# A spectral filter mixed with a token MLP: first weights on ScalarE's queue, two roots on ScalarE, second biases later, slots by their planes, last block in three pieces

## The chip, the cores and the metric

The kernel runs on one core of one Trainium2 chip. The metric is the device time of one execution in microseconds (us); the time before is the median of three runs, 129.3 us (129.15 to 129.92). The profile is of one execution, with all times counted from its first instruction. PE is TensorE's matmul stream, PEld its weight loads, DVE is VectorE, ACT is ScalarE, POOL is GpSimd, SP is SyncE, which here only issues transfers. A name with q (SPq, ACTq) is an engine's queue of issues.

## What is computed

The input x has 2048 rows of 512 columns in bf16. Two branches work on it and a gate per row mixes them.

```python
def _A_ref(x, w_r, w_i):
    X = rfft2(x.astype(float32)) * (w_r + 1j * w_i)
    return irfft2(X, s=(S, D)).astype(bfloat16)

def _B_ref(x, w1, b1, w2, b2):
    h = _layernorm(x, axis=-1)                       # (x - mean) / sqrt(var + 1e-5)
    u = _gelu(einsum("bsd,sf->bdf", h, w1) + b1)     # F = 1792
    y = einsum("bdf,fs->bds", u, w2) + b2
    return y.transpose(0, 2, 1)

g = _sigmoid((x * gate_w).sum(-1, keepdims=True))
return g * a + (1 - g) * b
```

## The kernel before, in words

The 2048 rows are 16 blocks of 128, one row to a partition. A block has the number b (0 to 15); "block 3 of x" is the one with b = 3.

**The MLP branch** is all matmuls of 128x128 weights against 512 columns. The first layer has 14 tiles of 128 features (ft), each the sum over the 16 blocks; 8 of them are made first, block after block as the normed blocks `hn` appear (`mm1`, L276, accumulators `u1`, weights `w1a`), the other 6 later from `w1b` (L446). The second layer makes each of 16 output blocks from 14 matmuls (L456, weights `w2t`, output `yb`); the last block is made apart, in two halves of columns (L785). ScalarE turns a first-layer tile into `gl` with gelu and the bias column `b1f` (L342), and evacuates each finished output block to `tbv` with the gate's scale and a bias `ombb2`, which is made from `b2f` (L436). The two bias vectors are loaded as rows into one tile `brow` (30 rows, L120 and L121) and turned to columns by one small matmul against a unit matrix (L240), which ScalarE copies to `bcol` (L294).

**The layer norm** of a block: DVE takes statistics (`bstat`, L247) and aggregates them (`aggr`, L254), adds epsilon (L256), POOL takes the power -1/2 (`rstd`, L259), and DVE scales the block (`norm_dve`, L272) for blocks 0 to 5; from block 6 on ScalarE scales (L268).

**The spectral branch** folds x by symmetries on DVE (L375 to L425) into planes `YA` and `YB`, for the even and the odd frequency groups A and B. PE transforms along the tokens (`token`, L504 and L505; 4 steps for a group, number r, each from planes 2r and 2r+1), ScalarE copies the result out (L506), PE transforms along the columns (`dpass`, L513), ScalarE copies again to `csA` or `csB` (L515), DVE applies the spectral weights and sums (L520 to L550, results `PMA` and `PMB`), and PE transforms back (`inv_tok`, L642, and `inv_d`, L658) with ScalarE copying between (L614). DVE unfolds the result (L690 to L758) into `ap`, which is added to the stored output by accumulating transfers from POOL's queue (L763) or, for blocks 12 to 14, by DVE (L772). The tables of sines (`TD`, `TA`) are made on the chip: POOL writes counters, DVE forms angles `md` and masks them (L205, L191), ScalarE takes sines (L194, L197).

**What sets the order.** Each engine runs its instructions in the order in which the code names them. A generator, `products`, holds the 96 + 210 = 306 MLP matmuls that follow the first eight tiles. `fill(n)` puts n of them into PE's order; `fill_to(t)` puts them until a planned clock reaches t. The clock starts at 33.2 and goes on by 0.2165 for each product and by `spent` for the transforms (0.87 a token step, 0.44 a column step). The constants `T_TA`, `T_TB`, `T_IA`, `T_IB`, `T_Y` (L24) are the planned times at which tokens A, tokens B, inverse A, inverse B and the unfolding come. They decide only the order on PE, and with it the order of ScalarE's evacuations, not a wait.

**The loads** are issued by SP in the order of L118 to L139: block 0 of x, then x and `w1a` blocks in turn, the gate's row `gwb`, the rest of `w1a`, `w1b` and the spectral weights. ACT's queue issues only the two bias rows. A transfer signals one of eight completion counters, taken in turn, and an issue waits for the earlier transfer that used its counter.

**The start of PE** is a row of warm-up matmuls on zeros (L241), nine of them, with the bias matmul behind the seventh. `pw` and `pb` share the two slots of the tag "mm" with `u1_6` and `u1_7`; the eighth tile's first matmul waits for the bias copy.

Of the kernel before, what the change touches and what calls it, by code (L numbers as in the profile page):

```python
# [20 lines left out]
NFT = 14  # L21
FT1 = 8
NDVE = 6
T_TA, T_TB, T_IA, T_IB, T_Y = 42.2, 55.4, 69.8, 82.6, 99.8  # L24
PI_IN = 3.1415925
INV_SCALE = 2.0 / (512.0 * 2048.0)
C1 = float(np.cos(np.pi / 8))
# [16 lines left out]
def kernel(  # L44
# [13 lines left out]
    nc = tc.nc  # L58
# [5 lines left out]
    small = ctx.enter_context(tc.tile_pool(name="small", bufs=1))  # L64
# [9 lines left out]
    def pair(name):  # L74
        return psum.tile([P, 2, 512], F32, tag="pair", name=name, bufs=3)
# [11 lines left out]
    w1b, w2t = {}, {}  # L87

    def load_x(b0, b1):
        nc.sync.dma_start(out=xh[b0 // 8][:, b0 % 8:(b1 - 1) % 8 + 1], in_=xv[:, b0:b1])  # L90

    def load_w1a(b0, b1):
        nc.sync.dma_start(out=w1a[b0 // 4][:, b0 % 4:(b1 - 1) % 4 + 1], in_=w1v[:, b0:b1, 0:FT1 * P])

    def load_w(i):

# [19 lines left out]
        nc.sync.dma_start(out=w2t[c][:], in_=w2v[:, :, c * 256:(c + 1) * 256])  # L116

    load_x(0, 1)  # L118
    brow = small.tile([NFT + NB, P], BF16, name="brow")
    nc.scalar.dma_start(out=brow[0:NFT], in_=B_b1.rearrange("(ft f) -> ft f", f=P))  # L120
    nc.scalar.dma_start(out=brow[NFT:NFT + NB], in_=B_b2.rearrange("(b a) -> b a", a=P))  # L121
    for b in range(3):
        load_x(b + 1, b + 2)
        load_w1a(b, b + 1)
    load_x(4, 6)
    load_w1a(3, 4)
    load_x(6, 8)
# [4 lines left out]
    load_w1a(8, 12)  # L132
    gwb = small.tile([P, D], BF16, name="gwb")
    nc.sync.dma_start(out=gwb[:], in_=gate_w[None, :].to_broadcast([P, D]))
    load_w1a(12, 16)
    load_w1b(0, 4)
    load_w1b(1, 5)
# [2 lines left out]

    warm = small.tile([P, P], BF16, name="warm")
    nc.vector.memset(warm[:], 0.0)
    consts = small.tile([P, 5], F32, name="consts")
    nc.vector.memset(consts[:, 0:1], -PI_IN)
    nc.vector.memset(consts[:, 1:2], PI_IN)
    nc.vector.memset(consts[:, 2:3], -0.5)  # L146
    nc.vector.memset(consts[:, 3:4], 0.0)
    nc.vector.memset(consts[:, 4:5], 1536.0)
    c_mpi, c_pi, c_mhalf = consts[:, 0:1], consts[:, 1:2], consts[:, 2:3]

    lrow = H(4, [P, 3, P], "lrow", F32)
# [9 lines left out]
    iota(lrow[:, 0:2], [[0, 2], [2, P]], 0)  # L161
    iota(lrow[:, 2], [[2, P]], 1)
    nc.gpsimd.memset(lrow[:, 1, 0:1], 256.0)
    ident = small.tile([NFT + NB, NFT + NB], BF16, name="ident")
    idf = small.tile([NFT + NB, NFT + NB], F32, name="idf")
    iota(idf[:], [[1, NFT + NB]], 0, -1)
    nc.gpsimd.tensor_single_scalar(ident[:], idf[:], 0.0, op=Alu.is_equal)
    iota(krow[:, 0], [[8, 2], [16, 64]], 0)
    iota(krow[:, 1], [[16, P]], 6)
# [20 lines left out]
    def mask(m, n):  # L190
        nc.vector.tensor_single_scalar(m, m, n - 1, op=Alu.bitwise_and)  # L191
# [8 lines left out]
    ma = [H(7, [P, 8, P], "ma0", I32), H(8, [P, 8, P], "ma1", I32)]  # L200
    mc = small.tile([P, 1], I32, name="mc")

    def angles_d():
        for v in range(2):
            nc.vector.tensor_scalar(md[:, v], lrow[:], acol[:, 1:2], 768.0 * v, op0=Alu.mult, op1=Alu.add)  # L205
        mask(md[:], 1024)

    def sines_d():
        nsin(TD[:, :, 1], md[:, 1], 1024)
        nsin(TD[:, :, 2], md[:, 0], 1024)  # L210
        psin(TD[:, :, 0], md[:, 0], 1024)
# [23 lines left out]

    pw = bank("pw")
    pb = bank("pb")
    for n in range(9):
        if n == 7:
            nc.tensor.matmul(pb[:, 0:NFT + NB], lhsT=brow[:], rhs=ident[:], start=True, stop=True)  # L240
        nc.tensor.matmul(pw[:].rearrange("p (n k) -> p n k", n=4), lhsT=warm[:],  # L241
                         rhs=warm[:, None, :].to_broadcast([P, 4, P]), start=True, stop=True)
    pu = [pair(f"u1_{i}") for i in range(3)]
# [2 lines left out]
    def bstat(b):  # L246
        nc.vector.bn_stats(out=stats[:, b, :], in_=xh[b // 8][:, b % 8, :])  # L247
# [4 lines left out]
    def aggr(b0, b1):  # L252
        for b in range(b0, b1):
            nc.vector.bn_aggr(out=mv[:, b, :], in_=stats[:, b, :])  # L254
        eng = nc.vector if on_dve(b0) else nc.gpsimd
        eng.tensor_scalar(mv[:, b0:b1, 1], mv[:, b0:b1, 1], 1e-5, 0.0, op0=Alu.add, op1=Alu.add)  # L256
        if not on_dve(b0):
            nc.gpsimd.tensor_scalar(nmr[:, b0:b1], mv[:, b0:b1, 0], -1.0, 0.0, op0=Alu.mult, op1=Alu.add)
        nc.gpsimd.tensor_tensor(rstd[:, b0:b1], mv[:, b0:b1, 1], c_mhalf.to_broadcast([P, b1 - b0]), op=Alu.pow)  # L259
# [24 lines left out]
    def gacc(b0, b1):  # L284
        for b in range(b0, b1):
            junk = small.tile([P, D], BF16, tag="junk", name="junk")
            nc.scalar.activation(junk[:], prod[b // 8][:, b % 8], ActF.Copy, accum_out=glog[:, b:b + 1])  # L287

    sink = small.tile([P, 1], F32, name="sink")
    nc.scalar.activation(sink[:], consts[:, 2:3], ActF.Sin, bias=c_mpi, scale=0.0)  # L290
    angles_d()
    sines_d()
    bcol = small.tile([P, NFT + NB], F32, name="bcol")
    nc.scalar.copy(bcol[:], pb[:, 0:NFT + NB])  # L294
    b1f, b2f = bcol[:, 0:NFT], bcol[:, NFT:]
    for v in range(2):
        nc.scalar.activation(ma[v][:], krow[:], ActF.Identity, bias=consts[:, 3 + v:4 + v], scale=acol[:, 0:1])
    nc.scalar.activation(mc[:], acol[:, 0:1], ActF.Identity, bias=consts[:, 4:5], scale=1024.0)


    bstat(0)
    aggr(0, 1)
    for b in range(NDVE):
        bstat(b + 1)
        norm_dve(b)
        if b + 1 < NDVE:
            aggr(b + 1, b + 2)
# [162 lines left out]
    def hook(b):  # L470
        store(b)

    clock = [33.2]
    act = [0.0]

    def fill(n):
        for _ in range(n):
            if next(prods, 0) == 0:
                return
            done[0] += 1  # L480
            clock[0] += 0.2165
# [69 lines left out]

    gacc(0, 4)
    fill(16)
    gacc(4, 7)
    fill(16)
    gacc(7, 10)
# [13 lines left out]
        fill(4)  # L570
    fill_to(T_TB)
    ZB = H(6, [P, 4, 4, 2, P], "ZB")
    for r in range(4):
        token(1, r, ZB, YB)
        spent(0.87)
        if r % 2:
            gacc(14 + r // 2, 15 + r // 2)
        fill(2)
    g_ = small.tile([P, NB], F32, name="g_")
    nc.scalar.activation(g_[:], glog[:], ActF.Tanh, scale=0.5)  # L580
# [5 lines left out]
    nc.gpsimd.tensor_mul(ombb2[:], omg[:], b2f)  # L586
    gate["omg"], gate["ombb2"] = omg, ombb2
    csB = H(4, [P, 4, 4, 256], "csB")
    for r in range(4):
        dpass(r, ZB, csB)  # L590
        spent(0.44)
        fill(3)
# [185 lines left out]
    fill(10000)  # L778

    b = NB - 1  # L780
    for h in range(2):
        hs = slice(256 * h, 256 * h + 256)
        y = bank("yb")
        for ft in range(NFT):
            nc.tensor.matmul(y[:, 0:256], lhsT=w2t[b // 2][:, ft, P:2 * P], rhs=gl[:, ft, hs],  # L785
                             start=(ft == 0), stop=(ft == NFT - 1))
        nc.vector.scalar_tensor_tensor(tbv[0][:, b, hs], y[:, 0:256], omg[:, b:b + 1], apl[:, hs],
                                       op0=Alu.mult, op1=Alu.add)
        nc.sync.dma_start(out=out2[b * P:(b + 1) * P, hs], in_=tbv[0][:, b, hs])

# [26 lines left out]
```

## Time and profile before

| | us |
|---|---|
| median of three runs | 129.3 |
| the profiled execution, device time | 129.32 |
| its span, first to last instruction | 127.4 |
| first matmul of `mm1` starts | 5.21 |
| PE's last matmul ends | 123.98 |
| last DVE operation ends | 124.49 |
| PE busy, DVE busy, ACT busy | 121.7, 111.0, 87.1 |

The span leaves out 1.9 us around the program. PE's busy time counts the tail of each matmul too, so that a matmul of 512 columns shows as 0.379 while the next starts 0.216 behind it; starts are the better measure. In a line of the timeline the first number is the start, the second the time covered, and the bracket tells how long the engine sat idle and what ended that. In the list of waits stand the waiting engine and line, what it waited for, the total, the times and the longest. A matmul's weight load (PEld) runs ahead of the matmul, so a wait on PEld costs PE only what goes beyond the work still in its queue. Transfers show the time from the start of their issue to their landing where somebody waited for them.

### The profile page before, as it was taken

How to read it: one execution, taken by the hardware profiler on the slowest of the kernel's cores; microseconds unless marked ns; L12 is line 12 of the kernel's file. 1: busy time of each engine (PE TensorE's matmuls, PEld its weight loads, DVE VectorE, ACT ScalarE, POOL GpSimd, SP SyncE). 2: the span in 40 equal slices, each digit the busy share in tenths (PEclk: the TensorE clock that was granted, in tenths of full speed). 3: DMA queues.
4: the chain of work that ended last, by engine and by line, in shares of the span. 5: the costliest groups of instructions: out<-in, count | busy, mean ns of one | idle time of the engine just before them, and what ended most of it. 6: DMA issues, size and time to landing. Idle time of an engine off the chain costs nothing.

```text
span 127.4 us, 2027 instructions
## 1 busy us (share of the span) xinstructions
PE 121.7 (95%) x723; PEld 64.5 (51%) x736; DVE 111.0 (87%) x188; ACT 87.1 (68%) x132; POOL 42.5 (33%) x69
## 2 busy tenths in 40 slices
PE   6999999999999999999999999999999999999990
PEld 2244444444444576447654765477544444444470
DVE  5969998999999999999999999999999999981130
ACT  4930359999897879959992599269764699322420
POOL 7633288998898595000220000000000000530300
PEclk9999999999999999999999999999999999999999
DMA  3799999999999999999399008510012111199691
GB/s 98 228 355 371 376 367 353 279 312 268 217 264 244 249 293 292 290 290 290 78 262 287 25 0 233 184 41 0 0 41 79 49 44 41 41 142 197 101 230 32
DMA packets 34490, 24.03 MB, mean 189 GB/s; under 512 B 5264, under 2 KB 31888, under 8 KB 34480
## 3 DMA queue, kind: packets, MB, share of 16 engines
q1 hardware_dynamic: 32340, 21.01, 60.7%
q0 software_dynamic: 1936, 2.76, 11.9%
q10 hardware_dynamic: 204, 0.14, 0.3%
q8 instruction: 5, 0.08, 0.3%
q14 instruction: 5, 0.04, 0.1%
HBM read 19.15 MB, written 3.67 MB: 179 GB/s over the span
## 4 chain that ended last, share of the span: by engine, by line
PE 53%; DVE 33%; DMA 4%; issue 3%; SPq 2%; POOL 2%; DVEq 0%
PE yb L456 35%; PE ivt L642 5%; DVE stats L247 4%; DMA xa<-in_A_x_dram 4%; DVE prod L280 4%; PE ivd L658 3%; PE u L446 3%; PE yb L785 2%; POOL rstd L259 2%; DVE F L379 2%; DVE s L388 2%; DVE T L375 2%; DVE o L407 2%; DVE F L380 2%; DVE T L376 2%
## 5 line engine op out<-in xcount | busy, mean ns | idle before, releaser
L456 PE MATMUL yb<-gl,w2t 128*128 128x512 bf16 x204 | 46.1, 379 | 0.3
L456 PEld LDWEIGHTS <-w2t 128*128 128x128 bf16 x210 | 20.2, 98 | 22.3
L276 PE MATMUL u<-hn,w1a 128*128 128x512 bf16 x126 | 27.9, 380 | 0.1
L446 PE MATMUL u<-hn,w1b 128*128 128x512 bf16 x91 | 22.4, 379 | 0.2
L436 ACT ACTIVATE tbv<-yb,ombb,omg 128x512 bf16<-128x512 f32 x15 | 11.7, 777 | 14.8 <-PE yb L456 14.8
L763 POOL DMA_DIRECT2D out_dram<-ap x3 | 4.0, 1527 | 51.0 <-DVE ap L758 45.2
L276 PEld LDWEIGHTS <-w1a 128*128 128x128 bf16 x128 | 12.5, 98 | 15.9 <-DMA w1a<-in_B_w_dram 0.9
L446 PEld LDWEIGHTS <-w1b 128*128 128x128 bf16 x96 | 9.1, 98 | 7.9
L287 ACT ACTIVATE junk<-prod 128x512 bf16<-128x512 bf16 x16 | 10.1, 630 | 0.3
L342 ACT ACTIVATE gl<-u,bcol 128x512 bf16<-128x512 f32 x14 | 9.3, 688 | 1.2 <-PE u L446 0.6
L614 ACT CAST R<-ivt 128x1024 bf16<-128x1024 f32 x8 | 7.8, 1038 | 3.4 <-PE ivt L642 3.4
L259 POOL TENSOR_TENSOR rstd<-mv,consts 128x1 f32<-128x1 f32 (+1 forms) x11 | 7.2, 653 | 6.5 <-DVE mv L256 6.3
L614 ACT CAST H<-ivd 128x1024 bf16<-128x1024 f32 x7 | 7.0, 1045 | 0.8 <-PE ivd L658 0.8
L772 DVE TENSOR_TENSOR tbv<-tbv,ap 128x512 bf16<-128x512 bf16 x3 | 1.3, 425 | 6.7 <-ACT tbv L436 6.7
L268 ACT ACTIVATE hn<-xb,nmr,rstd 128x512 bf16<-128x512 bf16 x8 | 6.0, 803 | 1.3 <-POOL nmr L263 1.3
L268 ACT ACTIVATE hn<-xa,nmr,rstd 128x512 bf16<-128x512 bf16 x2 | 1.5, 806 | 7.3 <-DVE nmr L265 7.3
L247 DVE BATCH_NORM_STATS2 stats<-xa 128x6 f32<-128x512 bf16 x8 | 5.5, 686 | 0.9 <-DMA xa<-in_A_x_dram 0.9
L535 DVE TENSOR_TENSOR tatb<-PMA,wn 128x1024 bf16<-128x1024 bf16 x8 | 5.0, 690 | 0.2 <-issue 0.2
L247 DVE BATCH_NORM_STATS2 stats<-xb 128x6 f32<-128x512 bf16 x8 | 5.2, 675 | 0.0
L241 PE MATMUL pw<-warm 128*128 128x512 bf16 x9 | 4.2, 628 | 1.0 <-DVE consts L146 1.0
L658 PEld LDWEIGHTS <-R 128*128 128x128 bf16 x64 | 3.8, 98 | 2.5 <-ACT R L614 2.5
L658 PE MATMUL ivd<-TI,R 128*128 128x128 bf16 x64 | 4.9, 220 | 0.1
(189 smaller groups left out, 224.1 us busy)
## 6 DMA issues: line engine op xcount, KB each, us to landing
w2t<-in_B_w_dram SPq DMA_DIRECT2D x8, 896.0 KB, 10.0
w1b<-in_B_w_dram SPq DMA_DIRECT2D x3, 1024.0 KB, 16.6
w1a<-in_B_w_dram SPq DMA_DIRECT2D x2, 1024.0 KB
out_dram<-tbv SPq DMA_DIRECT2D x14, 128.0 KB, 2.5
out_dram<-ap POOLq DMA_DIRECT2D x3, 512.0 KB, 6.2
w1a<-in_B_w_dram SPq DMA_DIRECT2D x4, 256.0 KB, 2.8
w1a<-in_B_w_dram SPq DMA_DIRECT2D x2, 512.0 KB, 6.5
xb<-in_A_x_dram SPq DMA_DIRECT2D x2, 512.0 KB, 7.2
```

Of the source, the lines that this page charges most:

```text
L247: nc.vector.bn_stats(out=stats[:, b, :], in_=xh[b // 8][:, b % 8, :])
L259: nc.gpsimd.tensor_tensor(rstd[:, b0:b1], mv[:, b0:b1, 1], c_mhalf.to_broadcast([P, b1 - b0]), op=Alu.pow)
L268: nc.scalar.activation(hn[:, b, :], xh[b // 8][:, b % 8, :], ActF.Identity, bias=nmr[:, b:b + 1], scale=rstd[:, b:b + 1])
L276: nc.tensor.matmul(u1[ft], lhsT=w1a[b // 4][:, b % 4, ft * P:(ft + 1) * P], rhs=hn[:, b, :], start=(b == 0), stop=(b == NB - 1))
L287: nc.scalar.activation(junk[:], prod[b // 8][:, b % 8], ActF.Copy, accum_out=glog[:, b:b + 1])
L342: nc.scalar.activation(gl[:, ft, :], src, ActF.Gelu_apprx_tanh, bias=b1f[:, ft:ft + 1], scale=1.0)
L436: nc.scalar.activation(tbv[0][:, b], y[:], ActF.Identity, bias=gate["ombb2"][:, b:b + 1], scale=gate["omg"][:, b:b + 1])
L446: nc.tensor.matmul(u[:], lhsT=w1b[c][:, b, k * P:(k + 1) * P], rhs=hn[:, b, :], start=(b == 0), stop=(b == NB - 1))
L456: nc.tensor.matmul(y[:], lhsT=w2t[b // 2][:, ft, (b % 2) * P:(b % 2 + 1) * P], rhs=gl[:, ft, :], start=(ft == 0), stop=(ft == NFT - 1))
L614: nc.scalar.copy(out, pr[:].rearrange("p h n -> p (h n)"))
L642: nc.tensor.matmul(o[:, 2 * v:2 * v + 2], lhsT=UV[:, 2 * v + c, r, par::2], rhs=TB[:, s, c:c + 2], start=(c == 0), stop=(c == 1))
L658: nc.tensor.matmul(pr[:, c, o * P:(o + 1) * P], lhsT=plane(par, cos), rhs=TI[:, lst, t], start=True, stop=True)
```

## The change

It has seven parts.

- `load_w1a` of block 0 goes out on ACT's queue, at the second place of the code; the order on SP becomes x0, x1, w1, x2, w2, x3, x4 and 5, w3, and on.
- The bias rows become two tiles. The first (`brow`) stays on ACT's queue, behind the first weights. The second (`brow2`) is issued by SP behind the gate's row; its matmul (`pb2`, with the accumulator of a pair slot) and ScalarE's copy come behind the first 16 products.
- Eight warm-up matmuls instead of nine.
- For blocks 0 and 1 the norm's root moves: ScalarE takes the square root of variance plus epsilon and DVE the reciprocal, in place of DVE's add and POOL's power. This needs ScalarE's table for roots, loaded by a dummy ahead, and then the one for sines, by another dummy.
- The angles of `TD` are masked behind block 1's scaling instead of ahead of block 0's statistics, and its sines come behind the two `ma` and the `mc` operations.
- Tokens B and their column transforms run in the order of r = 3, 1, 0, 2 instead of 0, 1, 2, 3. The plan's constants change: `T_TA` 42.2 to 42.7, `T_TB` 55.4 to 55.2, the clock's start 33.2 to 32.8.
- The last output block is made in pieces of 256, 128 and 128 columns instead of 256 and 256, each with its DVE operation and its store.

```diff
-T_TA, T_TB, T_IA, T_IB, T_Y = 42.2, 55.4, 69.8, 82.6, 99.8
+T_TA, T_TB, T_IA, T_IB, T_Y = 42.7, 55.2, 69.8, 82.6, 99.8
...
     def load_w1a(b0, b1):
-        nc.sync.dma_start(out=w1a[b0 // 4][:, b0 % 4:(b1 - 1) % 4 + 1], in_=w1v[:, b0:b1, 0:FT1 * P])
+        (nc.scalar if b0 == 0 else nc.sync).dma_start(out=w1a[b0 // 4][:, b0 % 4:(b1 - 1) % 4 + 1], in_=w1v[:, b0:b1, 0:FT1 * P])
...
     load_x(0, 1)
-    brow = small.tile([NFT + NB, P], BF16, name="brow")
-    nc.scalar.dma_start(out=brow[0:NFT], in_=B_b1.rearrange("(ft f) -> ft f", f=P))
-    nc.scalar.dma_start(out=brow[NFT:NFT + NB], in_=B_b2.rearrange("(b a) -> b a", a=P))
-    for b in range(3):
+    load_w1a(0, 1)
+    brow = small.tile([NFT, P], BF16, name="brow")
+    brow2 = small.tile([NB, P], BF16, name="brow2")
+    nc.scalar.dma_start(out=brow[:], in_=B_b1.rearrange("(ft f) -> ft f", f=P))
+    load_x(1, 2)
+    for b in range(1, 3):
+        load_w1a(b, b + 1)
         load_x(b + 1, b + 2)
-        load_w1a(b, b + 1)
...
     nc.sync.dma_start(out=gwb[:], in_=gate_w[None, :].to_broadcast([P, D]))
+    nc.sync.dma_start(out=brow2[:], in_=B_b2.rearrange("(b a) -> b a", a=P))
...
+    nc.vector.memset(consts[:, 5:6], 1e-5)
...
-    for n in range(9):
+    for n in range(8):
         if n == 7:
-            nc.tensor.matmul(pb[:, 0:NFT + NB], lhsT=brow[:], rhs=ident[:], start=True, stop=True)
+            nc.tensor.matmul(pb[:, 0:NFT], lhsT=brow[:], rhs=ident[0:NFT, 0:NFT], start=True, stop=True)
...
     sink = small.tile([P, 1], F32, name="sink")
+    nc.scalar.activation(sink[:], consts[:, 5:6], ActF.Sqrt, bias=consts[:, 5:6], scale=1.0)
+    for v in range(2):
+        nc.vector.tensor_scalar(md[:, v], lrow[:], acol[:, 1:2], 768.0 * v, op0=Alu.mult, op1=Alu.add)
+    def root(b):
+        nc.vector.bn_aggr(out=mv[:, b, :], in_=stats[:, b, :])
+        nc.scalar.activation(rstd[:, b:b + 1], mv[:, b, 1:2], ActF.Sqrt, bias=consts[:, 5:6], scale=1.0)
+    bcol = small.tile([P, NFT + NB], F32, name="bcol")
+    b1f, b2f = bcol[:, 0:NFT], bcol[:, NFT:]
+    for b in range(2):
+        bstat(b)
+        root(b)
+        if b == 0:
+            nc.scalar.copy(b1f, pb[:, 0:NFT])
+        else:
+            bstat(2)
+        nc.vector.reciprocal(rstd[:, b:b + 1], rstd[:, b:b + 1])
+        norm_dve(b)
+    mask(md[:], 1024)
     nc.scalar.activation(sink[:], consts[:, 2:3], ActF.Sin, bias=c_mpi, scale=0.0)
-    angles_d()
-    sines_d()
-    bcol = small.tile([P, NFT + NB], F32, name="bcol")
-    nc.scalar.copy(bcol[:], pb[:, 0:NFT + NB])
-    b1f, b2f = bcol[:, 0:NFT], bcol[:, NFT:]
     for v in range(2):
         nc.scalar.activation(ma[v][:], krow[:], ActF.Identity, bias=consts[:, 3 + v:4 + v], scale=acol[:, 0:1])
     nc.scalar.activation(mc[:], acol[:, 0:1], ActF.Identity, bias=consts[:, 4:5], scale=1024.0)
-    bstat(0)
-    aggr(0, 1)
-    for b in range(NDVE):
+    sines_d()
+    aggr(2, 3)
+    for b in range(2, NDVE):
         bstat(b + 1)
         norm_dve(b)
...
-    clock = [33.2]
+    clock = [32.8]
...
     fill(16)
+    pb2 = pair("pb2")
+    nc.tensor.matmul(pb2[:, 0, 0:NB], lhsT=brow2[:], rhs=ident[:], start=True, stop=True)
+    nc.scalar.copy(b2f, pb2[:, 0, 0:NB])
     gacc(4, 7)
...
-    for r in range(4):
+    for n, r in enumerate((3, 1, 0, 2)):
         token(1, r, ZB, YB)
...
-    for r in range(4):
+    for r in (3, 1, 0, 2):
         dpass(r, ZB, csB)
...
-    for h in range(2):
-        hs = slice(256 * h, 256 * h + 256)
+    for h0, h1 in ((0, 256), (256, 384), (384, 512)):
+        hs = slice(h0, h1)
         y = bank("yb")
         for ft in range(NFT):
-            nc.tensor.matmul(y[:, 0:256], lhsT=w2t[b // 2][:, ft, P:2 * P], rhs=gl[:, ft, hs],
+            nc.tensor.matmul(y[:, 0:h1 - h0], lhsT=w2t[b // 2][:, ft, P:2 * P], rhs=gl[:, ft, hs],
                              start=(ft == 0), stop=(ft == NFT - 1))
-        nc.vector.scalar_tensor_tensor(tbv[0][:, b, hs], y[:, 0:256], omg[:, b:b + 1], apl[:, hs],
+        nc.vector.scalar_tensor_tensor(tbv[0][:, b, hs], y[:, 0:h1 - h0], omg[:, b:b + 1], apl[:, hs],
                                        op0=Alu.mult, op1=Alu.add)
```

More of the change, by code (lines that the diff above doesn't have):

```diff
@@ L142 @@
     nc.vector.memset(warm[:], 0.0)
-    consts = small.tile([P, 5], F32, name="consts")
+    consts = small.tile([P, 6], F32, name="consts")
     nc.vector.memset(consts[:, 0:1], -PI_IN)
@@ L163 @@
     nc.gpsimd.memset(lrow[:, 1, 0:1], 256.0)
-    ident = small.tile([NFT + NB, NFT + NB], BF16, name="ident")
-    idf = small.tile([NFT + NB, NFT + NB], F32, name="idf")
-    iota(idf[:], [[1, NFT + NB]], 0, -1)
+    ident = small.tile([NB, NB], BF16, name="ident")
+    idf = small.tile([NB, NB], F32, name="idf")
+    iota(idf[:], [[1, NB]], 0, -1)
     nc.gpsimd.tensor_single_scalar(ident[:], idf[:], 0.0, op=Alu.is_equal)
@@ L201 @@
     mc = small.tile([P, 1], I32, name="mc")
[L203 to L206, printed above, removed]
     def sines_d():
@@ L572 @@
     ZB = H(6, [P, 4, 4, 2, P], "ZB")
-    for r in range(4):
+    for n, r in enumerate((3, 1, 0, 2)):
         token(1, r, ZB, YB)
         spent(0.87)
-        if r % 2:
-            gacc(14 + r // 2, 15 + r // 2)
+        if n % 2:
+            gacc(14 + n // 2, 15 + n // 2)
         fill(2)
```

## The prediction, written before the changed kernel had run

> **What bounds the kernel now.** I read the page's head first, then the waits, then the chain and the timeline around the places that the waits name, and last the busy time by stretches.
>
> ```profile
> PE 121.7 (95%) x723; PEld 64.5 (51%) x736; DVE 111.0 (87%) x188; ACT 87.1 (68%) x132; POOL 42.5 (33%) x69
> ```
>
> TensorE looks like the only bound. The stretches say more (columns: stretch, its length, then busy time of PE, PEld, DVE, ACT, POOL):
>
> ```profile
> 9.00:22.00 13.00, 12.95 (x60) 5.74 (x60) 11.94 (x37) 5.95 (x8) 7.82 (x19) 1.00 1.06 364
> 22.00:83.00 61.00, 59.92 (x400) 33.70 (x406) 59.77 (x79) 51.22 (x84) 25.50 (x29) 1.00 0.93 229
> 114.00:127.40 13.40, 9.97 (x61) 5.67 (x58) 2.47 (x6) 2.94 (x4) 1.27 (x1) 1.00 0.80 143
> ```
>
> From 22 to 83 us VectorE is busy 59.77 of 61.00, as full as TensorE: two chains run side by side and meet where PE needs what DVE made. The waits name the meetings:
>
> ```profile
> PE tok L504 <- DVE YA L401: 0.4, 1, 0.4
> PE tok L505 <- DVE YB L425: 0.3, 1, 0.3
> PEld L642 <- DVE PMB L545: 0.3, 1, 0.3
> DVE stats L247 <- DMA xa<-in_A_x_dram: 0.9, 2, 0.7
> ```
>
> The third is the one that counts. It is the last meeting, before the inverse transform of the second half:
>
> ```profile
> 82.80 0.21 DVE L545 COPY PMB<-YwB 128x16 bf16<-128x16 bf16 x1
> 83.06 1.00 PEld L642 LDWEIGHTS <-PMB 128*128 128x128 bf16 x10 [0.31 <-DVE PMB L545]
> 83.09 1.15 PE L642 MATMUL ivt<-TB,PMB 128*128 128x256 bf16 x9
> ```
>
> The weight load waited to the copy's end at 83.01; the matmul stream behind it lost nothing, since its queue ended at 83.09. So DVE and PE arrive here at one time, and from here PE runs without a hole to 123.98. The DVE side, followed back, starts with the loads of x:
>
> ```profile
> 4.03 4.95 DMA xa<-in_A_x_dram
> 8.97 0.02 issue
> 8.99 0.69 DVE stats L247
> ...
> 120.91 3.07 PE yb L785 x28
> 123.98 0.03 issue
> 124.01 0.48 DVE tbv L787
> ```
>
> Between 8.99 and 83 us that side is DVE work and GpSimd roots that wait for each other. The time is thus: the moment at which DVE has finished PMB, plus 40.89 us of matmuls (83.09 to 123.98), plus the tail of 3.4 us to 127.4. The profiled execution took 129.32 us with this span of 127.4; the median of the runs is 129.3, so one sum serves both.
>
> **Part 1, the front on PE.** Moving the first weights to ACT's queue takes one issue (0.42) off SP: the loads behind are issued up to 0.94 earlier: the weights of block 1 at 1.66 for 2.60, those of block 2 at 2.60 for 3.55. Block 3 of x stays at 3.08, now behind the weights of block 2. Blocks 4 and 5 of x come at 3.55 for 4.03, or when the first weights have landed (4.5 today), since they take over that load's completion counter. One warm-up matmul less is 0.43. Block 0's chain today: statistics 2.95, aggregate 3.67, add 3.89, root on POOL 4.13 to 4.71, scaling 4.75 to 5.16, first matmul 5.21. New, from a start s of the statistics: aggregate s+0.72, root on ACT s+0.94 to 1.22 (0.28, from the 128x1 ACTIVATE of L298), reciprocal s+1.26 to 1.41 (no row; bounds 0.06, a memset, and 0.58, POOL's root; I take 0.15, the 128x1 DVE add), scaling s+1.45, first matmul s+1.91. With s near 3.1 PE starts at 5.0 instead of 5.21. That is worth nothing at the end: ahead of the meeting PE also loses its holes at YA and YB, because tokens A come four products later and tokens B use the planes in the order in which DVE writes them. The holes are 0.16, 0.58 and 0.44, from the starts of neighbouring matmuls in the timeline (41.88 to 42.26, 44.02 to 44.82, 55.49 to 56.04) less a matmul's own 0.216 or 0.109: 1.2 together. Against this stand two more products (0.43), the second biases' matmul (0.06) and a product block whose evacuation on ACT (0.78, L436) now stands ahead of an inverse's copy and can hold PE 0.35 near 74. So PE would reach the meeting at about 83.09 - 0.2 - 1.2 + 0.43 + 0.06 + 0.35 = 82.5, and DVE is not there before 83. The cover of all PE edits is this wait of about 0.5; up to that much, a late start or late scaled blocks (1 and 2 come 0.1 to 0.2 late for PE by the steps below) cost nothing, beyond it they cost in full.
>
> **Part 2, the front on DVE.** This sets the end one for one. Steps from s: the mask (0.56) moves from before s to behind block 1; block 1's statistics s+1.77, its aggregate s+2.49, its root on ACT to s+2.98, block 2's statistics s+2.62, reciprocal s+3.23, scaling s+3.42, mask s+3.75, aggregate 2 s+4.23, add s+4.44, POOL root s+4.68 to 5.23, block 3's statistics s+4.51, scaling 2 s+5.27, aggregate 3 s+5.59, add s+5.80, POOL root s+6.03 to 6.58, scaling 3 s+6.62, aggregate 4 s+6.95. Aggregate 4 stands at 9.92 today, and from there the order is unchanged. So DVE moves by s - 2.97. Two other clocks: block 3's statistics to aggregate 4 is 2.29 without a wait, so x block 3 may land until 7.63 (today 7.53); and x blocks 4 and 5 until 8.99 (today 8.97).
> What is s? Block 0 of x lands at 0.72 + 2.1 = 2.82 today; the mask ahead of it is gone, DVE is free at 2.44. At best s is 2.85. At worst all 256 KB of the first weights go first: at the 271 GB/s of 2 to 3 us that is 0.97, so 3.79. I take 3.1, nearer the low end, because the engines moved only 0 to 106 GB/s until 2.0 and had room. For x block 3, 256 KB more ahead of it cost at most 0.70 at the 365 GB/s of 7 to 8 us (8.23), and at least nothing less the earlier start (7.1); I take 7.7. Both give DVE +0.1 us.
>
> **Part 3, two more products ahead of the meeting.** The plan's clock starts at 32.8 for 33.2 while T_IB stays 82.6, so the changed order has 158 product matmuls ahead of this inverse instead of 156. Behind it are 2 x 0.216 = 0.43 us less.
>
> **Part 4, the last block.** Two pieces of 14 matmuls at 256 columns take 3.07. Eight matmuls of 128x128 take 0.45 (L513, L658), 0.056 each with their weight loads, so the pieces of 256, 128, 128 take 1.53 + 1.57: +0.03. The last DVE operation falls from 0.48 to about 0.36 (128x1024 from PSUM takes 1.21, so 0.95 ns a column): -0.12. The last store shrinks from 64 to 32 KB: today 2.0 from issue to landing; bounds 1.7, the shortest of the stores, and 2.5, the 128 KB ones; I take no change.
> [...]
>
> **Part 5, what is hidden.** ACT has a second table load (1.28) and a dummy (0.29), and the sines come later: ACT sits idle 7.34 us ahead of its scaling at 14.73 today. The pb copy needs the first biases, which now queue behind the first weights on ACT's ring; the copy stands ahead of block 1's root, needed at s+2.7 = 5.8, copy today 4.78: 1 us of cover. If that goes, block 1's reciprocal and all DVE behind it wait. SP's new issue of the second biases (0.33) stands ahead of the last w1a load and w1b, whose issue of 11.38 us is held by the transfers. The copy of the second biases (0.16) is for ombb2, whose input comes at 62.6.
>
> **Sum.** 129.32 - 0.43 + 0.10 + 0.03 - 0.12 = 128.9.
>
> **Rivals.**
> A, the first weights hold up x block 0 (slower side). Both transfers start at 0.72. Place: the statistics of block 0. Price: s - 2.97 on DVE, one for one. It decides from s = 3.49 (0.43 + 0.12 - 0.03 used up). For it: 2 to 3 us already runs at 0.99 DMA share. Against: only half of the weights need to go ahead if they alternate. At s = 3.79: 129.32 - 0.52 + 0.82 = 129.6. [...]
> B, x block 3 comes late behind the third weights: landing 8.23, DVE +0.60, time 129.4. For it: DMA moved only 109 GB/s from 5 to 6 us, unexplained, and that could come again; against: no load is issued later than today but the last w1a and w1b.
> [...]
> D, PE alone decides: 0.2 earlier, 0.25 more if s is 2.85, 1.2 of holes gone, 0.1 of tail: 129.32 - 1.75 = 127.6. For it: 95% PE. Against: the load at 83.06 waits for DVE's copy, and nothing in the change shortens DVE after 9.92.
> E, something late on ACT (table load, biases) holds block 1's root by 2 us or more: 130.9. Against: the cover above.
>
> **How the numbers follow.** Likeliest case 0.55 (128.4 to 129.2), A 0.17, B 0.13, C 0.05, D 0.05, E 0.05. The predicted time is 128.9. Low end: s = 2.85 (-0.12), store 0.3 shorter: 129.32 - 0.43 - 0.12 + 0.03 - 0.12 - 0.3 = 128.4. High end: A with a store 0.2 longer: 129.8. A measurement of this kernel tells about 1% (1.3 us) from no change; only D is faster by that (0.05), only E slower (0.05); the rest, 0.90, is within it.
>
> **What would show it.** Right: the wait of L545's successor before the second inverse grows to 0.5 us or more and names DVE; the waits on YA L401 and YB L425 are gone; 40.5 us from that inverse to PE's end; the last DVE operation 0.36. The step on s is read from the first statistics, that on x block 3 from the wait ahead of the fourth. Wrong: PE enters the second inverse without waiting, or that inverse moves by more than the first aggregates did.

## The result and the profile after

The changed kernel is about 1% slower: 130.87 us median of four runs (130.65 to 131.25) against 129.54 of the kernel before on the same chip, a ratio of 1.0106 with a 95% interval of 1.0077 to 1.0136. The profiled execution took 131.02 with a span of 129.2, against 129.32 and 127.4. The forecast was 128.9. Ratios here and below leave out a few disturbed, slower runs, which the medians hold.

In the changed kernel L275 is `mm1`, L246 `bstat`, L253 and L295 the aggregates, L296 ScalarE's root, L271 `norm_dve`, L560 the last copy to PMB, L660 `inv_tok`, L805 the last DVE operations and L807 their stores. First the engines' line of the page after, then three of its waits (total, times, longest; lines between them are left out):

```profile
PE 123.6 (96%) x750; PEld 65.7 (51%) x750; DVE 111.5 (86%) x190; ACT 89.9 (70%) x137; POOL 38.3 (30%) x67
```

```profile
PEld L275 <- issue: 3.9, 11, 1.2
...
DVE stats L246 <- DMA xa<-in_A_x_dram: 1.6, 2, 1.2
...
PE u L275 <- DVE hn L271: 0.7, 1, 0.7
```

PE's waits for YA and YB are gone, as forecast. Its wait for PMB, which was forecast to grow to 0.5 or more, is gone too. In their place stand longer waits of DVE for x at the front, a wait of PE's first layer for the scaled block 0, and eleven waits of the first layer's weight loads, with which PE's slow pace there shows (matmuls 0.427 apart, below). DVE's front, from the timeline after (start, time, bracket with the idle time before and what ended it):

```profile
3.61 0.69 DVE L246 BATCH_NORM_STATS2 stats<-xa 128x6 f32<-128x512 bf16 x1 [1.20 <-DMA xa<-in_A_x_dram]
4.34 0.18 DVE L295 BATCH_NORM_AGGREGATE mv<-stats 128x2 f32<-128x6 f32 x1
4.88 0.17 DVE L307 RECIPROCAL rstd<-rstd 128x1 f32<-128x1 f32 x1 [0.36 <-ACT rstd L296]
...
6.68 0.70 DVE L246 BATCH_NORM_STATS2 stats<-xa 128x6 f32<-128x512 bf16 x1 [0.37 <-DMA xa<-in_A_x_dram]
...
11.03 0.18 DVE L253 BATCH_NORM_AGGREGATE mv<-stats 128x2 f32<-128x6 f32 x1
```

Block 0 of x landed at 3.58 (0.72 + 2.86 in the chain), where the prediction had read 2.82 for the kernel before, and DVE then waited again, for block 2. As the statistics of block 2 stand ahead of block 1's reciprocal in the code, that wait held block 1 back too: its reciprocal started at 7.29 (with w0 on SP at 6.08). Aggregate 4, from which the order is unchanged, came at 11.03 instead of 9.92. PE lost time of its own. The busy time in the stretch of 4.05 us from the first `mm1` matmul on (stretch, length, then PE, PEld, DVE, ACT and POOL with the number of instructions in brackets), after:

```profile
5.55:9.60 4.05, 4.05 (x10) 1.47 (x10) 3.47 (x10) 3.22 (x5) 0.58 (x1) 1.00 0.98 327
```

and the equal stretch before:

```profile
5.21:9.26 4.05, 4.05 (x20) 1.84 (x19) 2.96 (x11) 2.19 (x3) 1.47 (x3) 1.00 0.90 302
```

Both look fully busy, but the first holds half the matmuls: they start 0.427 apart instead of 0.216, at half clock, up to 9.6. The clock column (third from the end) shows 1.00 in both and does not tell; the count does. The trace's record of the granted clock has full speed from 9.60 on after and from 5.43 on before. The meeting at the second inverse and the end, from the timeline after:

```profile
84.15 0.21 DVE L560 COPY PMB<-YwB 128x16 bf16<-128x16 bf16 x1
...
84.71 1.30 PEld L660 LDWEIGHTS <-PMB 128*128 128x128 bf16 x11
...
84.93 1.25 PE L660 MATMUL ivt<-TB,PMB 128*128 128x256 bf16 x10
...
124.40 2.43 SPq L807 DMA_DIRECT2D out_dram<-tbv  x3
...
125.45 0.35 DVE L805 SCALAR_TENSOR_TENSOR tbv<-yb,omg,ap 128x128 bf16<-128x128 f32 x1 [0.43 <-PE yb L803]
```

The copy ends at 84.36, 1.35 later than before; the load has no bracket, since PE came later still, at 84.93 (before 83.09). From there to PE's end are 40.48 us (before 40.88), and from PE's end to the span's end 3.83 (before 3.45). So the span grew by 1.84 - 0.40 + 0.38 = 1.8: the meeting is late, the plan's gain came, the tail got longer. Both of the prediction's signs of being wrong are there: PE enters the second inverse without waiting, and the inverse moved by 1.84 where aggregate 4 moved by 1.11 (9.92 to 11.03).

### The profile page after: what moved, and what is told of

It is laid out like the page before. It is cut to its first block, busy times and chain, and to the rows that moved or that the text cites. A ratio compares the mean times of both kernels' runs of the same rounds, so it can differ in the third digit from the quotient of the medians.

```text
span 129.2 us, 2074 instructions
## 1 busy us (share of the span) xinstructions
PE 123.6 (96%) x750; PEld 65.7 (51%) x750; DVE 111.5 (86%) x190; ACT 89.9 (70%) x137; POOL 38.3 (30%) x67
## 4 chain that ended last, share of the span: by engine, by line
PE 90%; ACT 3%; DMA 2%; DVE 1%; issue 0%
PE yb L471 34%; PE u L275 23%; PE u L461 16%; PE ivt L660 4%; PE dp L528 3%; PE yb L803 2%; PE tok L520 2%; PE tok L519 2%; DMA xa<-in_A_x_dram 2%; PE ivd L676 2%; ACT R L632 1%; ACT H L632 1%; DVE stats L246 1%; ACT tbv L451 1%; PE tok L516 0%; DVE hn L271 0%
## 5 line engine op out<-in xcount | busy, mean ns | idle before, releaser
L471 PE MATMUL yb<-gl,w2t 128*128 128x512 bf16 x210 | 47.5, 379 | 0.0
L275 PE MATMUL u<-hn,w1a 128*128 128x512 bf16 x128 | 29.8, 398 | 0.7 <-DVE hn L271 0.7
L461 PE MATMUL u<-hn,w1b 128*128 128x512 bf16 x96 | 23.3, 379 | 0.0
L275 PEld LDWEIGHTS <-w1a 128*128 128x128 bf16 x128 | 13.1, 102 | 17.6 <-issue 3.9
L258 POOL TENSOR_TENSOR rstd<-mv,consts 128x2 f32<-128x2 f32 (+1 forms) x9 | 6.1, 677 | 9.1 <-DVE mv L255 9.0
L246 DVE BATCH_NORM_STATS2 stats<-xa 128x6 f32<-128x512 bf16 x8 | 5.5, 687 | 1.6 <-DMA xa<-in_A_x_dram 1.6
L246 DVE BATCH_NORM_STATS2 stats<-xb 128x6 f32<-128x512 bf16 x8 | 5.2, 676 | 0.0
L550 DVE TENSOR_TENSOR tatb<-PMB,wn 128x2048 bf16<-128x2048 bf16 x4 | 4.7, 1227 | 0.2
L521 ACT CAST ZA<-tok 128x1024 bf16<-128x1024 f32 x4 | 4.0, 1018 | 1.2 <-PE tok L520 1.1
```

What stands on the lines that cost most here:

```text
L275: nc.tensor.matmul(u1[ft], lhsT=w1a[b // 4][:, b % 4, ft * P:(ft + 1) * P], rhs=hn[:, b, :], start=(b == 0), stop=(b == NB - 1))
L461: nc.tensor.matmul(u[:], lhsT=w1b[c][:, b, k * P:(k + 1) * P], rhs=hn[:, b, :], start=(b == 0), stop=(b == NB - 1))
L471: nc.tensor.matmul(y[:], lhsT=w2t[b // 2][:, ft, (b % 2) * P:(b % 2 + 1) * P], rhs=gl[:, ft, :], start=(ft == 0), stop=(ft == NFT - 1))
L550: mul(tt[:, i, :, r:r + n], PM[:, 2 * s:2 * s + 2, r:r + n], w[:, None].to_broadcast([P, 2, n, 256]))
```

## The experiments

Two theories stood at the start. *Transfers*: the new order of loads makes DVE late, and DVE sets the meeting. *Clock*: the hole between the last warm-up (over at about 4.63, its start at 4.20 plus the 0.427 of a matmul) and the first `mm1` matmul (5.55) keeps PE at half clock, and PE sets it. For the tail, a third: *the stores* of 256-byte rows, of which SP took 1.30 us to issue one (the others 0.33 and 0.38). All ratios are against the kernel before, on the same chip. "w0" are the weights of block 0.

| kernel | median us | ratio (95%) |
|---|---|---|
| ten warm-ups | 130.73 | 1.0099 (1.0061 to 1.0137) |
| w0 on SP | 129.68 | 1.0008 (0.9980 to 1.0036) |
| both | 129.53 | 0.9997 (0.9967 to 1.0027) |
| both, two halves | 129.64 | 1.0009 (0.9977 to 1.0041) |
| tail alone | 129.70 | 1.0021 (0.9989 to 1.0052) |
| plan alone | 129.49 | 0.9976 (0.9943 to 1.0009) |
| loads alone | 131.19 | 1.0134 (1.0080 to 1.0189) |
| w0 on SP, two halves | 129.24 | 0.9966 (0.9932 to 0.9999) |
| x2 first | 130.52 | 1.0043 (1.0006 to 1.0079) |
| w0 behind biases, two halves | 129.65 | 0.9976 (0.9934 to 1.0018) |
| second store by ACT | 129.63 | 1.0003 (0.9975 to 1.0032) |
| w0 on SP, two halves, 160 ahead | 128.88 | 0.9942 (0.9908 to 0.9976) |
| the same with 384 and 128 columns | 128.62 | 0.9944 (0.9914 to 0.9974) |
| 160 ahead, two halves, more rows on PE | 128.69 | 0.9919 (0.9888 to 0.9951) |

### Ten warm-ups

```diff
-    for n in range(8):
+    for n in range(10):
```

> The changed kernel with ten warm-up matmuls instead of eight, so that PE is busy from its first warm-up until about 5.5 us. Clock theory (the hole of 0.9 us ahead of the first layer keeps TensorE at half speed until 9.6 us and that is the loss): first-layer matmuls come 0.216 apart from about 6.2 us at the latest, and the time falls by the whole 1.8 us of the span's growth, to about 129.1. Transfer theory (the loads make DVE 1.35 us late at the last meeting, and the slow PE only hides that): the clock is mended all the same, PE then waits for DVE at the second inverse, which starts at about 84.4 instead of 84.9, and the time falls by 0.5 to about 130.4.

Full clock now came at 6.93, later than the 6.2 expected, which was the author's estimate and rests on no trace, and the meeting reads (timeline of this kernel):

```profile
83.98 0.21 DVE L560 COPY PMB<-YwB 128x16 bf16<-128x16 bf16 x1
...
84.24 0.77 PEld L660 LDWEIGHTS <-PMB 128*128 128x128 bf16 x8 [0.90 <-DVE PMB L560]
84.25 0.94 PE L660 MATMUL ivt<-TB,PMB 128*128 128x256 bf16 x7 [0.41 <-DVE PMB L560]
```

The kind of wait that the kernel before had is back, and larger: PE stands idle 0.41 for DVE. The median hardly moved (130.73 for 130.87). Mending the clock alone uncovers DVE's delay; the transfer theory's number was nearer.

### The first weights back on SP's queue

```diff
     load_x(0, 1)
-    load_w1a(0, 1)
...
-    load_x(1, 2)
-    for b in range(1, 3):
-        load_w1a(b, b + 1)
+    for b in range(3):
         load_x(b + 1, b + 2)
+        load_w1a(b, b + 1)
```

with `load_w1a` on SP for all blocks (two kernels, one with eight warm-ups and one with ten).

> The changed kernel with the first weights back on SP's queue and the loads in the order of before; eight warm-ups and all else stay. Transfer theory: block 0 of x lands at 2.8 instead of 3.6 and block 2 no longer late, statistics start at 2.85, first layer at 4.8 so that the hole behind the warm-ups is only 0.15 and the clock comes at 5.4 to 6.2; DVE reaches the second inverse at about 82.9; time 129.3 to 129.5, of which 0.36 is the longer tail. Clock theory alone (eight warm-ups are too few by themselves): the half speed until 9.6 stays and the time stays above 130.3.

> Both edits: ten warm-ups, and the first weights on SP's queue with the old order of loads. Ten warm-ups end near 5.5 and so start the first layer 0.7 later than the kernel with eight could, which by the transfer theory is covered as long as DVE comes last at the second inverse: time equal to that of the kernel with loads alone put back within 0.2, 129.3. If PE comes last there, up to 0.5 more.

Statistics started at 2.88 and 2.91, aggregate 4 came at 9.82 and 9.86, PMB was ready at 83.08 and 83.11, the second inverse began at 83.13 and 83.17. That takes 1.2 to 1.3 of the 1.33 us away, with eight warm-ups as with ten: with eight the first layer now starts at 4.85, and full clock came at 4.11, ahead of it. The loads are the main cause. What is left shows the tail: PE ended at 123.63 in the first, earlier than before (123.97), and yet the span was 128.2.

### The last block, and the loads alone

Both edits with the last block in two halves:

> As the kernel with both edits, and the last block in two halves again. Tail theory (the store of short rows takes SP 1.3 us to issue and holds the last store): span end minus PE's end goes back from 3.78 to 3.4, time 0.36 less than with three pieces, 128.9. By the prediction's step on the last block (pieces gain 0.12 in the last DVE operation, lose 0.03 on PE): 0.1 more than with three pieces.

```diff
-    for h0, h1 in ((0, 256), (256, 384), (384, 512)):
+    for h0, h1 in ((0, 256), (256, 512)):
```

And the reverse, only the three pieces, put into the kernel before:

> The kernel before with only the last block in pieces of 256, 128 and 128 columns. Tail theory (the stores of 256-byte rows hold SP's queue: 1.3 us for one issue in the changed kernel, and the last store starts behind it): PE's end to span's end 3.8 to 4.5 instead of 3.44, time +0.4 to +0.7, 130.0 to 130.2. The prediction's step on the last block: -0.1.

The tail is as the theory had it, 3.45 with halves, 3.97 and 3.81 with three pieces. The medians do not follow so clearly: 129.64 against 129.53 for the first pair, where in the profiled execution with halves full clock came at 6.96 instead of 6.11 and PE reached the meeting 0.43 later. Tail alone is +0.2% with an interval that holds no change; block 3 of x was also late there (fourth statistics 8.01, before 7.53).

The loads alone:

> The kernel before with only the first weights on ACT's queue and the changed order of loads; the nine warm-ups, the mask ahead of block 0's statistics and POOL's roots stay. Transfer theory as it stands after the first four runs: block 0 of x lands at 3.6, block 2 at 6.6; the kernel before has 0.91 us of waits for blocks 3 and 4 that the delay eats first, so aggregate 4 comes at 10.35 (+0.43) and the time is +0.4, 130.0. If the delay of block 0 and block 2 counts in full, aggregate 4 at 11.0 and +1.1, 130.7.

This is `load_w1a(0, 1)` on ACT's queue and the changed order of loads, put into the kernel before. It was slower than either number, 131.19, and for another reason. DVE was only 0.15 late at aggregate 4 (10.07) and had PMB at 83.19. But both bias rows now queued behind the first weights, and PE's order has the bias matmul ahead of the last warm-ups (timeline, loads alone):

```profile
5.45 0.18 PE L242 MATMUL pb<-ident,brow 30*128 30x30 bf16 x1 [1.30 <-POOL rstd L261]
5.56 1.03 PE L243 MATMUL pw<-warm 128*128 128x512 bf16 x2
6.38 1.06 PE L278 MATMUL u<-hn,w1a 128*128 128x512 bf16 x2
```

The bracket names POOL, which this matmul does not read; what it reads is `brow`. PE stood still about 1.5 us in its warm-up, full clock came at 8.85, and the second inverse began at 84.28, 1.1 behind PMB. Here PE carries the loss: its first layer starts 1.17 late (6.38 for 5.21), and its first ten matmuls, most of them at half clock, take 3.39 where the kernel before took 2.25. On DVE the delay of block 0 is eaten by the 0.91 us of waits for blocks 3 and 4 that the kernel before has.

### The plan alone, and the sum without loads and tail

> The kernel before with only the plan's constants and the order of tokens B. By the prediction's step on the plan: the waits at YA and YB go (1.2 us of holes on PE), PE still waits for DVE's PMB at the second inverse at 83.1 with two more products behind it, time -0.43 against before. Rival: PE and DVE were level at the meeting, the holes return as other waits, and the two products push the meeting back by 0.43: no change.

```diff
-T_TA, T_TB, T_IA, T_IB, T_Y = 42.2, 55.4, 69.8, 82.6, 99.8
+T_TA, T_TB, T_IA, T_IB, T_Y = 42.7, 55.2, 69.8, 82.6, 99.8
-    clock = [33.2]
+    clock = [32.8]
-    for r in range(4):
+    for n, r in enumerate((3, 1, 0, 2)):
         token(1, r, ZB, YB)
```

And the changed kernel with w0 on SP and two halves (both edits shown above):

> The changed kernel with the first weights back on SP's queue in the old order, and the last block in two halves; eight warm-ups, ScalarE's roots, later second biases, plan and tokens-B order stay. If loads and tail are the whole loss and the plan's gain of 0.43 and DVE's 0.12 are real: 129.0. If the plan's gain is not real: 129.4 to 129.6, like the kernel before.

From the second inverse to PE's end it was 40.47 in both, 0.41 less than before; PE still waited for DVE at the meeting (0.21 and 0.27). The second gains 0.34%, the first 0.24% with an interval that just holds no change (its tail was 4.12, though it has two halves). In both traces the plan's gain is there, near the 0.43; the times alone do not settle it for the first, and the second also has the moved roots and biases.

### What made x late

Block 2 of x ahead of the weights of block 1, with ten warm-ups:

> The changed kernel with ten warm-ups, and on SP's queue block 2 of x ahead of the weights of block 1 (x0, x1, x2, w1, x3, w2); the first weights stay on ACT's queue. If DVE's delay of 1.1 at aggregate 4 is two delays, 0.64 from block 0 of x and the rest from block 2: block 0 still lands at 3.6, block 2 by 6.2, aggregate 4 comes at 10.55 (3.6 + 6.95) instead of 10.9 with ten warm-ups alone, time 130.4. If block 2's place on SP does not matter (the delay is all from the first weights): 10.9 and 130.7. If all of it is block 2: 9.9 and 129.7.

```diff
     load_x(1, 2)
-    for b in range(1, 3):
-        load_w1a(b, b + 1)
-        load_x(b + 1, b + 2)
+    load_x(2, 3)
+    load_w1a(1, 2)
+    load_x(3, 4)
+    load_w1a(2, 3)
```

From its timeline, DVE only:

```profile
3.68 0.69 DVE L247 BATCH_NORM_STATS2 stats<-xa 128x6 f32<-128x512 bf16 x1 [1.27 <-DMA xa<-in_A_x_dram]
...
6.30 0.66 DVE L247 BATCH_NORM_STATS2 stats<-xa 128x6 f32<-128x512 bf16 x1
...
10.62 0.17 DVE L254 BATCH_NORM_AGGREGATE mv<-stats 128x2 f32<-128x6 f32 x1
```

The wait for block 2 is gone, and aggregate 4 stands 6.94 behind the first statistics, where the prediction's steps had 6.95. In the changed kernel they were 7.42 apart. So DVE's delay is two delays: about 0.64 from block 0 and 0.47 from block 2, which lands behind the weights of block 1.

w0 still on ACT's queue, but behind the first biases, with two halves:

> The changed kernel with the first weights still on ACT's queue but behind the first biases, so issued 0.65 later than block 0 of x, and with the last block in two halves; SP's order is that of the change. If it is the two transfers starting together that hold block 0 of x: it lands at 2.8 to 3.1. If what is first on a queue does not matter and the transfers share to the end: 3.4 or later. What then sets the time is block 2 of x, which stays behind the weights of block 1: if it still lands at 6.6, aggregate 4 comes at 11.0 and the time is 130.4; if it lands by 5.6, 9.9 and 129.3.

```diff
     load_x(0, 1)
-    load_w1a(0, 1)
     brow = small.tile([NFT, P], BF16, name="brow")
     brow2 = small.tile([NB, P], BF16, name="brow2")
     nc.scalar.dma_start(out=brow[:], in_=B_b1.rearrange("(ft f) -> ft f", f=P))
+    load_w1a(0, 1)
```

From its timeline, DVE only:

```profile
2.89 0.69 DVE L246 BATCH_NORM_STATS2 stats<-xa 128x6 f32<-128x512 bf16 x1 [0.47 <-DMA xa<-in_A_x_dram]
...
5.77 0.69 DVE L246 BATCH_NORM_STATS2 stats<-xa 128x6 f32<-128x512 bf16 x1 [0.18 <-DMA xa<-in_A_x_dram]
...
10.12 0.17 DVE L253 BATCH_NORM_AGGREGATE mv<-stats 128x2 f32<-128x6 f32 x1
```

The same queue, the same order on SP, the weights issued at 1.41 instead of 0.73: block 0 lands in time, and block 2 with it at about 5.75. Both delays go when the two large transfers no longer start together. The packets of the changed kernel show the sharing: from 2 to 3 us ACT's queue moved 182 KB of the first weights and SP's queue 95 KB of x, where SP's had moved 239 KB in the kernel before; by 3.5 all 256 KB of the weights had moved, and block 0 landed just after. Why block 2 lands 0.9 earlier here, with the same transfers queued ahead of it, is not shown. The ratio, 0.9976, cannot be told from no change, and is 1.3% under the changed kernel's; the halves are a part of that.

### The tail

The second of three stores on ACT's queue, in the kernel with w0 on SP:

> The kernel with the first weights back on SP's queue and the last block in three pieces, with the store of the second piece issued by ACT's queue instead of SP's. Tail theory (the second store's long issue holds the third on the same queue): PE's end to span's end falls from 3.9 to 4.5 to about 3.3, time 129.1, at or under the kernel with two halves (129.24). If the stores of short rows are slow wherever they are issued: 3.9 or more and 129.6.

```diff
-        nc.sync.dma_start(out=out2[b * P:(b + 1) * P, hs], in_=tbv[0][:, b, hs])
+        (nc.scalar if h0 == 256 else nc.sync).dma_start(out=out2[b * P:(b + 1) * P, hs], in_=tbv[0][:, b, hs])
```

The last issues took 0.33 and 0.34, and the tail was 3.91. So the tail can be long without a long issue. The kernel with w0 on SP, which has no long issue either, shows where the time is: its last store was issued by 124.38. Its busy time in stretches of a microsecond (last two columns: busy share of the 16 DMA engines, GB/s):

```profile
123.50:124.50 1.00, 0.13 (x3) 0.00 (x0) 0.35 (x1) 0.00 (x0) 0.00 (x0) 1.00 1.19 265
124.50:125.50 1.00, 0.00 (x0) 0.00 (x0) 0.00 (x0) 0.00 (x0) 0.00 (x0) 1.00 0.43 104
125.50:126.50 1.00, 0.00 (x0) 0.00 (x0) 0.00 (x0) 0.00 (x0) 0.00 (x0) 1.00 0.06 13
```

The same stretches of the kernel with w0 on SP and two halves, whose last store was issued by 124.72:

```profile
124.50:125.50 1.00, 0.00 (x0) 0.00 (x0) 0.00 (x0) 0.00 (x0) 0.00 (x0) 1.00 0.41 119
125.50:126.50 1.00, 0.00 (x0) 0.00 (x0) 0.00 (x0) 0.00 (x0) 0.00 (x0) 1.00 0.01 2
```

In the first, a share of 0.06 for a whole microsecond is one engine of sixteen at work, alone. One line of the table of its queues (packets, MB, share) between 123.7 and 126.5 stands out:

```profile
...
q8 instruction: 1, 0.02, 2.2%
```

This is one packet of 16 KB in the queue that the profile names instruction, called the fetch from here on; it started at 124.27 and took 0.98 us, and the rows of the last stores that fall to its engine stood behind it. From 125.23 to 126.36 the packet record has, one behind the other, 8 packets of 1024 bytes, 8 of 512 and 16 of 256: a sixteenth of the rows of each of the last four stores.

The changed kernel has such a fetch from 124.88 to 125.97, and there it goes with the long issue. Two lines of its timeline, SP only:

```profile
125.05 1.30 SPq L807 DMA_DIRECT2D out_dram<-tbv  x1
...
126.44 0.38 SPq L807 DMA_DIRECT2D out_dram<-tbv  x1
```

The issue of the second store ended 0.38 behind the fetch, so the last store, whose data was ready at 125.80, was issued at 126.44, about 0.6 late, and its packets ran last, on all engines. With ten warm-ups, with both edits and in tail alone it was the last store's own issue that was long: 0.83, 0.98 and 0.82, each ending 0.36 behind the fetch. In those four traces the tail is long through the issue; in the other four with a fetch there, through the rows behind it. Why an issue should wait for the fetch is not shown: two that began during one took 0.33 (plan alone, second store by ACT).

The page of the changed kernel counts six packets in the queue of fetches:

```profile
q8 instruction: 6, 0.10, 0.3%
```

and the page before five:

```profile
q8 instruction: 5, 0.08, 0.3%
```

Over all sixteen profiled executions, by when the last fetch ran:

| fetch of 16 KB | kernels | PE's end to span's end |
|---|---|---|
| starts from 0.6 ahead of PE's end to 0.7 behind it | changed, ten warm-ups, w0 on SP, both, tail alone, x2 first, second store by ACT (all three pieces); plan alone (halves) | 3.81 to 4.54 |
| none there | before, both with halves, loads alone, w0 on SP with halves, w0 behind | 3.44 to 3.45 |
| over by 123.45, ahead of the last store | 160 ahead, more rows | 3.44 |
| none there, 384 and 128 | 384 and 128 columns | 3.21 |

Two runs were made to tell short rows from the fetch:

Short rows without more instructions on PE:

> The fastest kernel so far (first weights on SP's queue, plan's clock from 32.4) with the last block in pieces of 384 and 128 columns: as many matmuls and weight loads on PE as with two halves, but the last store has 128 rows of 256 bytes as with three pieces. Short-row theory (stores of 256-byte rows land late): PE's end to span's end 3.8 to 4.5, as in all seven traces with three pieces, and time 129.3 or more. Instruction-fetch theory (the 28 more matmul and load instructions bring a sixth 16 KB fetch of PE's program, which holds one DMA engine for 1 us among the last stores): no fetch among the last stores, tail 3.3, time 128.8.

```diff
-    for h0, h1 in ((0, 256), (256, 512)):
+    for h0, h1 in ((0, 384), (384, 512)):
```

More instructions on PE without short rows:

> The fastest kernel so far, last block in two halves, with the sixth warm-up matmul replaced by 14 of 32 columns: 26 instructions more on PE, far from the tail, and no short rows. Instruction-fetch theory: the trace shows a sixth 16 KB instruction packet within 1 us of PE's end, the tail is 3.8 to 4.5 instead of 3.44, time 129.3 to 129.9. Short-row theory: tail 3.44 and time as before, 128.9 to 129.1 (the longer warm-up stretch may cost up to 0.3).

```diff
+        if n == 5:
+            for _ in range(14):
+                nc.tensor.matmul(pw[:, 0:32], lhsT=warm[:], rhs=warm[:, 0:32], start=True, stop=True)
+            continue
```

With 384 and 128 columns, from the timeline:

```profile
122.42 0.62 DVE L803 SCALAR_TENSOR_TENSOR tbv<-yb,omg,ap 128x384 bf16<-128x384 f32 x1 [1.04 <-PE yb L801]
123.06 0.85 SPq L805 DMA_DIRECT2D out_dram<-tbv  x2
123.20 0.35 DVE L803 SCALAR_TENSOR_TENSOR tbv<-yb,omg,ap 128x128 bf16<-128x128 f32 x1 [0.17 <-PE yb L801]
```

The last store has the same short rows, its issue took 0.33, and the tail is 3.21, the shortest of all: short rows are not the cause, neither of a long issue nor of a long tail. With more rows on PE the sixth fetch came inside the span, as expected, but at 122.44, early enough to be over before the last store, and the tail stayed at 3.44; that half of the expectation missed. What is shown: the tail is long where the fetch runs among the last stores, and in no other trace. What triggers it is not settled. Three pieces put 28 more instructions on PE, and the fetch then fell there in seven traces of seven; but with unchanged numbers of instructions it fell there once in the plan alone, and at 122.47 in the next kernel.

### Two more products ahead

> The kernel with the first weights back on SP's queue and two halves, with the plan's clock started at 32.4 instead of 32.8: two more products ahead of the second inverse. There PE waited 0.27 for DVE in the profiled execution. If DVE comes last at the meeting in nearly all executions: -0.27, about 129.0. If PE and DVE are level there: no change, 129.2 to 129.4.

```diff
-    clock = [32.8]
+    clock = [32.4]
```

The second inverse began at 83.24, with PMB at 83.06, and 40.02 us remained: 0.45 less again. The ratio 0.9942 is the first clearly faster one, and the same kernel with 384 and 128 columns, or with the longer warm-up, stays there (0.9944 and 0.9919). PE and DVE are level at the meeting now, within 0.2.

## Why the prediction was wrong

The prediction's span was 127.42 - 0.43 + 0.10 + 0.03 - 0.12 = 127.0; 129.24 was measured, 2.24 more.

- *What bounds it* held: the end is the meeting at the second inverse, plus 40.48, plus a tail. But PE, not DVE, came last to that meeting in this trace.
- *Part 2, s.* Taken 3.1 within 2.85 to 3.79; 3.61. The argument "nearer the low end, because the engines moved only 0 to 106 GB/s until 2.0 and had room" failed: that they were idle before 2.0 says nothing of the time in which both transfers are served, and there x got 95 KB of 277 from 2 to 3 us. All of the weights had moved by 3.5, near the worst bound. The term is mis-sized by 0.51. Rival A named this place and its point of decision (3.49), and that happened; its argument against itself, that only half of the weights need to go ahead, failed. Block 0 landed at 3.58 where both started at 0.72, and in time for statistics at 2.89 where the weights were issued at 1.41.
- *Part 2, block 2.* The chain of steps was right to 0.01 where no block was late (6.94 with w0 on SP, and with x2 first), but that "block 2's statistics [at] s+2.62" would find its data was not checked, though the change puts the weights of block 1 ahead of it and those of block 0 beside it. It landed at 6.66 and cost 0.47; with either of the two moved away the wait was gone or 0.18. The text watched blocks 3, 4 and 5 instead; rival B's block 3 was not waited for. Three traces with w0 on SP waited 0.24 to 0.58 for block 4 (with two halves, second store by ACT, more rows on PE), so x can come late there too.
- From aggregate 4 to PMB were 73.33 instead of 73.09 (kernels with the changed front: 73.2 to 73.3). These 0.2 were not traced further.
- *Part 1, PE.* "Up to that much, a late start ... cost nothing" left out the clock: with eight warm-ups full clock came at 9.60, with ten and the same loads at 6.93. One warm-up fewer and a later first block made a hole of 0.9; the first ten matmuls, at half clock, took 4.14 instead of 2.25, and PE came 0.52 behind even the late DVE. Part 1's own sum, with the start 0.34 late instead of 0.2 early and these 1.89 more, gives 83.09 + 0.34 + 1.89 - 1.2 + 0.43 + 0.06 + 0.35 = 84.96, and 84.93 was measured: what the sum lacked is the clock and the late start. In the medians little of this shows (130.87 and 130.73 with ten warm-ups); which engine came last in the unprofiled runs is not known. The stretches at full clock in the sixteen traces lasted 119.47 or 122.88 us, and in the five kernels with eight warm-ups and w0 on SP they began between 3.72 and 5.86, though these kernels are alike up to there; what sets the start is not shown.
- *Part 3* was right: 40.48 for 40.88, and 40.02 with two more.
- *Part 4.* PE's part was right (40.50 with three pieces, 40.45 to 40.47 with halves), and the last DVE operation too (0.35 for 0.36). "I take no change" for the store failed: the tail was 0.50 longer than forecast. The second store's issue took 1.30 while an instruction fetch ran, and the last store went out about 0.6 late; no bound there allowed for it. Without a fetch there the same short last store gave a tail of 3.21 (384 and 128 columns), under the 3.33 of the forecast.
- *Part 5* held: ScalarE's tables, the copies and the second biases cost nothing visible. But the bias rows' place in the queue mattered elsewhere: in the loads alone they stopped PE.

The terms: 0.51 + 0.47 + 0.24 + 0.52 + 0.50 = 2.24. The first two are the loads, the third is open, the fourth is PE's late start and half clock, which the late block 0 and the missing warm-up made together, and the last is the store held up while the fetch ran.

## What to carry to other kernels

A load moved to another queue was not extra room here: block 0 of x landed at 3.58 instead of 2.82. Check each transfer that starts beside it and each that stands behind it, up to the first one that had slack, and try issuing it a little later on the same queue (at 1.41 instead of 0.73 it let block 0's statistics start at 2.89). Read how long PE stands still between the last warm-up and the first real matmul: with 0.92 us here it ran at half clock until 9.60, and with two more warm-ups until 6.93. Where two engines meet, mending one can uncover the other (PE waited 0.41 for DVE with ten warm-ups); read both arrival times before saying what a wait costs.

## What was not expected of the hardware

In eight of sixteen traces a 16 KB instruction packet held one of the 16 DMA engines for 0.98 to 1.09 us among the last stores, and the tail was 0.4 to 1.1 longer than the 3.44 without it. No run here shows what starts the fetch. The issue of a 32 KB store on SP took 1.30, 0.98, 0.83 and 0.82 in four of these eight traces and 0.33 to 0.38 elsewhere; in the four it ended 0.36 to 0.38 behind the fetch, and the last packets were those of a store held up by it.
